# A depthwise-separable convolution on one core: pw in one transfer, x chunk 0 on ScalarE's queue, dummy matmuls up to pw's landing

## The chip, the cores and the metric

One core of a Trainium2 chip. The metric is the device time of an execution in microseconds. Two numbers occur: the **time** (575.14 us and so on), and the **span** of the same execution as its records show it. The time is 1.7 to 1.8 us longer than the span, so either can be used to compare kernels; I use spans where I take an execution apart.

## The reference

```python
H = W = 384; C = 384; k = 1                  # x: 1 x 384 x 384 x 384 bf16, dw: 1 x 1 x 384, pw: 384 x 384
out = xp[:, 0:H, 0:W, :] * dw[0, 0]          # k is 1: one scale for each channel
return jnp.einsum('bhwc,cd->bhwd', out, pw)
```

With k = 1 this is one matrix product, x (147,456 x 384) times diag(dw) pw. The kernel builds the weights w = diag(dw) pw once and then streams x through TensorE in 288 steps of 512 rows.

## The kernel before

The **prologue** makes the weights. dw is turned into a column by three tiny matmuls (L199), VectorE makes the scaled selection matrices `sel_w`, and TensorE multiplies them with pw (L218), in pairs of matmuls for the two halves of the rows. ScalarE and VectorE copy the six results from PSUM into `w_r`.

```python
nc.scalar.dma_start(dw_row[:], dw.rearrange("a e c -> a (e c)")).then_inc(s_dw, 16)
nc.sync.dma_start(pw_n[:, 0, :], pw[:P, :]).then_inc(s_pw[0], 16)
nc.sync.dma_start(pw_n[:, 1:3, :], pw[P:, :].rearrange("(k p) d -> p k d", p=P)).then_inc(s_pw[1], 16)
# ... then all loads of x and all stores, on the same SyncE queue, in the order in which they are due

nc.tensor.wait_ge(s_zero, 1)
idle_work(3)                      # dummies: 3 rounds of 4 matmuls on zeros, in a loop (L184)
# ... the three dw matmuls (L199)
idle_work(1)
times = {(1, 1): 3, (2, 0): 3}    # these build steps are repeated, only to keep TensorE busy
for k in range(3):
    if k < 2:
        nc.tensor.wait_ge(s_pw[k], 16)
    nc.tensor.wait_ge(s_sw, k + 1)
    for r in range(2):
        if k == 2:
            nc.tensor.wait_ge(*w_done[r])         # PSUM is used again: a copy must be done
        for v in [0, 1] * times.get((k, r), 1):
            mm = nc.tensor.matmul(...)            # L218: sel_w x pw_n
        mm.then_inc(s_w)
```

The **loop** has 48 matmuls a step (L167), after VectorE has transposed the rows of x and with ScalarE evicting the step before. And the last three loads of x have another layout, whose first dimension is only 4:

```python
if first + LONG < NS:                              # LONG = 3
    src = rows.rearrange("(p s) c -> p (s c)", p=P)
    dst = dst.rearrange("p s c -> p (s c)")
else:
    src = rows.rearrange("(a k q) c -> q a k c", k=4, q=4)
```

## Time and profile before

| | before |
|---|---|
| time, first three runs | 575.14 us (574.9 to 576.55) |
| span of the profiled run | 574.1 us |
| prologue, up to the loop's first matmul | 7.28 us |
| first eviction, last eviction | 9.80, 569.45 us |
| tail, last eviction to the end | 4.7 us |
| DMA, mean over the span | 395 GB/s |

The lines that carry this stand in the prediction below. Here are rows of the stretches of 1 us at the end of the kernel before, and SyncE's last wait for the stores. The last two figures of a stretch are the busy share of the 16 DMA engines and what they moved in GB/s.

```profile
571.00:572.00 1.00, 0.00 (x0) 0.00 (x0) 0.00 (x0) 0.00 (x0) 0.00 (x0) 1.00 0.68 267
572.00:573.00 1.00, 0.00 (x0) 0.00 (x0) 0.00 (x0) 0.00 (x0) 0.00 (x0) 1.00 0.32 126
573.00:574.00 1.00, 0.00 (x0) 0.00 (x0) 0.00 (x0) 0.00 (x0) 0.00 (x0) 1.00 0.00 0
```

```profile
SPq L142 <- DMA out_dram<-O: 2.0, 1, 2.0
```

No engine computes here any more. The last store drains at hundreds of GB/s, then nothing is left, and SyncE has waited 2.0 us for it. In this run the end was clean.

### The profile page before, as it was taken

The numbers are of one execution on the slowest core, as the hardware profiler recorded it, in microseconds if no ns is written. First come the engines' busy times: TensorE is split into PE (matmuls) and PEld (weight loads), VectorE is DVE, ScalarE is ACT, GpSimd is POOL, SyncE is SP. The second block draws the span as 40 slices with busy tenths as digits, with TensorE's granted clock in tenths as the row PEclk, the third lists the DMA queues.
The fourth block names the chain that finished last, engine by engine and source line by source line (L and its number), as shares of the span: only waits on it lengthen the run. The fifth ranks groups of instructions, "written<-read, shape, count | busy, mean of one in ns | idle before, by whom it ended". The sixth has DMA issues, their size and how long they took to land.

```text
span 574.1 us, 29692 instructions
## 1 busy us (share of the span) xinstructions
PE 567.5 (99%) x13863; PEld 334.3 (58%) x13863; DVE 508.2 (89%) x583; ACT 419.1 (73%) x296; POOL 0.9 (0%) x8
## 2 busy tenths in 40 slices
PE   8999999999999999999999999999999999999996
PEld 4555555555555555555555555555555555555553
DVE  7889888988988898899889888988988898899884
ACT  6777777777777777777777777777777777777775
POOL 0000000000000000000000000000000000000000
PEclk9999999999999999999999999999999999999999
DMA  8999999999999999999999999999999999995996
GB/s 327 442 404 408 431 415 423 436 429 405 383 411 412 391 400 428 398 390 402 426 385 400 398 430 403 390 393 419 396 395 424 400 388 392 421 397 172 414 386 241
DMA packets 25929, 226.88 MB, mean 395 GB/s; under 512 B 1214, under 2 KB 5695, under 8 KB 22079
## 3 DMA queue, kind: packets, MB, share of 16 engines
q1 hardware_dynamic: 25916, 226.79, 98.1%
q14 instruction: 10, 0.07, 0.0%
q8 instruction: 1, 0.02, 0.0%
q10 hardware_dynamic: 2, 0.00, 0.0%
HBM read 113.54 MB, written 113.25 MB: 395 GB/s over the span
## 4 chain that ended last, share of the span: by engine, by line
PE 98%; DMA 1%; ACT 0%; DVE 0%; SPq 0%; issue 0%
PE ps L167 97%; DMA pw_n<-in_pw_dram 1%; PE ps L218 0%; DMA out_dram<-O 0%; ACT O L309 0%; DVE O L306 0%; SPq L132 0%; SPq L339 0%; SPq L100 0%
## 5 line engine op out<-in xcount | busy, mean ns | idle before, releaser
L167 PE MATMUL ps<-w_r,T 32*128 32x384 bf16 x13824 | 562.2, 321 | 0.0
L260 DVE STREAM_TRANSPOSE T<-X 128x384 uint32<-128x384 uint32 x576 | 505.0, 878 | 56.0 <-DMA X<-in_x_dram 1.4
L309 ACT CAST O<-ps 128x1536 bf16<-128x1536 f32 x288 | 413.6, 1436 | 148.1 <-PE ps L167 148.1
L167 PEld LDWEIGHTS ps<-w_r,T 32*128 32x128 bf16 x13824 | 332.5, 93 | 229.9 <-issue 1.0
L273 ACT CAST w_r<-ps 128x768 bf16<-128x768 f32 x5 | 3.9, 800 | 1.5 <-PE ps L218 1.5
L218 PE MATMUL ps<-pw_n,sel_w 64*128 64x384 bf16 x20 | 3.6, 518 | 0.5 <-DVE sel_w L288 0.3
L306 DVE CAST O<-ps 128x768 bf16<-128x768 f32 x1 | 1.0, 957 | 3.0 <-DMA out_dram<-O 3.0
L184 PE MATMUL ps<-zero 32*128 32x384 bf16 x16 | 1.8, 493 | 1.4 <-POOL zero L234 1.4
L218 PEld LDWEIGHTS ps<-pw_n,sel_w 64*128 64x128 bf16 x20 | 1.2, 131 | 2.6 <-DMA pw_n<-in_pw_dram 1.5
L246 ACT ACT_TABLE_LOAD x1 | 1.3, 1283 | 1.5 <-SPq L100 1.5
L278 DVE TENSOR_REDUCE sel<-eye 128x64 f32<-128x128 bf16 x1 | 0.3, 289 | 1.8 <-POOL eye L236 1.8
L184 PEld LDWEIGHTS ps<-zero 32*128 32x128 bf16 x16 | 0.5, 99 | 2.0 <-issue 2.0
L273 DVE CAST w_r<-ps 128x768 bf16<-128x768 f32 x1 | 1.0, 958 | 0.5 <-PE ps L218 0.5
L288 DVE TENSOR_SCALAR sel_w<-sel,dw_f 128x256 bf16<-128x256 f32 x3 | 0.9, 350 | 0.0
L285 DVE COPY dw_f<-ps 128x3 f32<-128x3 f32 x1 | 0.2, 160 | 0.8 <-PE ps L199 0.8
L236 POOL TENSOR_SCALAR_AFFINE_SELECT eye<-ones 128x128 bf16<-128x128 bf16 x1 | 0.3, 292 | 0.1
L246 ACT COPY warm<-warm 128x1 f32<-128x1 f32 x2 | 0.3, 189 | 0.0
L199 PEld LDWEIGHTS ps<-ones,dw_row 1*128 1x128 bf16 x3 | 0.2, 100 | 0.2 <-issue 0.2
L234 POOL MEMSET zero<- 128x192 uint32 x1 | 0.3, 258 | 0.0
L199 PE MATMUL ps<-ones,dw_row 1*128 1x1 bf16 x3 | 0.2, 160 | 0.0
L235 POOL MEMSET ones<- 128x128 bf16 x1 | 0.2, 204 | 0.0
L328 POOL MEMSET const-bfloat16-1.0<- 128x1 bf16 x1 | 0.1, 102 | 0.0
(4 smaller groups left out, 0.4 us busy)
## 6 DMA issues: line engine op xcount, KB each, us to landing
X<-in_x_dram SPq DMA_DIRECT2D x26, 3840.0 KB, 21.6
out_dram<-O SPq DMA_DIRECT2D x26, 3840.0 KB, 27.6
X<-in_x_dram SPq DMA_DIRECT2D x2, 1536.0 KB, 17.2
out_dram<-O SPq DMA_DIRECT2D x2, 1536.0 KB, 13.8
X<-in_x_dram SPq DMA_DIRECT2D x3, 768.0 KB, 7.6
out_dram<-O SPq DMA_DIRECT2D x3, 768.0 KB, 10.7
X<-in_x_dram SPq DMA_DIRECT2D x1, 2304.0 KB, 19.4
out_dram<-O SPq DMA_DIRECT2D x1, 2304.0 KB, 11.3
```

The costliest lines, as they stand in the source:

```text
L167: mm = nc.tensor.matmul(PS[s][:, q, :D], lhsT=Ts[s][32 * q : 32 * q + 32, b, par::2], rhs=w_r[32 * q : 32 * q + 32, b, par, :], start=(b, ...
L184: nc.tensor.matmul(PS[0][:, i, :D], lhsT=zero[32 * i : 32 * i + 32, 0:P], rhs=zero[32 * i : 32 * i + 32, :], start=True, stop=True, tile_p ...
L199: mm = nc.tensor.matmul(PS[1][:, 0, D + k : D + k + 1], lhsT=dw_row[:, P * k : P * k + P], rhs=ones[0:1, 0:1], start=True, stop=True,)
L218: mm = nc.tensor.matmul(PS[(k + 1) % 2][:, 2 * r + v, :D], lhsT=sel_w[64 * v : 64 * v + 64, k, r, :, :].rearrange("p q w -> p (q w)"), rhs ...
L234: nc.gpsimd.memset(zero[:].bitcast(U32), 0).then_inc(s_zero)
L236: nc.gpsimd.affine_select(out=eye[:], in_=ones[:], pattern=[[-1, P]], compare_op=mybir.AluOpType.is_equal, fill=0.0, base=0, channel_multi ...
L246: c = nc.scalar.copy(warm[:, s + 1 : s + 2], warm[:, 0:1])
L260: ins = nc.vector.transpose(out=Tw[:, 3 * h : 3 * h + 3], in_=Xw[:, :, j, 96 * h : 96 * h + 96].rearrange("p k (b w) -> p b k w", w=32),)
L273: o = nc.vector.tensor_copy(out, in_) if e == 0 else nc.scalar.copy(out, in_)
L288: nc.vector.tensor_scalar_mul(sel_w[:, k], sel[:].unsqueeze(2).to_broadcast([P, 2, 4, 32]), dw_f[:, k : k + 1]).then_inc(s_sw)
L306: e = nc.vector.tensor_copy(Ov[:, nq:4, j, :], PS[s][:, nq:4, :D])
L309: a = nc.scalar.copy(Ov[:, 0:nq, j, :], PS[s][:, 0:nq, :D])
```

## The change

Its intent: save one DMA issue on SyncE, start x earlier on a second queue, and fill TensorE's gaps before pw lands, in the hope that TensorE's clock comes up sooner. What I call the clock is read in two ways that agree: the trace's record of the granted clock begins at 8.08 us in the profile before, and the loop's matmuls take 485 ns each at 7.95 to 8.1 us and 321 ns from 8.5 on.

```diff
-    s_pw = [nc.alloc_semaphore(f"s_pw{h}") for h in range(2)]
+    s_pw = nc.alloc_semaphore("s_pw")
@@
-        def load_x(t):
+        def load_x(t, eng=nc.sync):
@@
-            nc.sync.dma_start(dst, src).then_inc(s_x[g % NR][i], 16)
+            eng.dma_start(dst, src).then_inc(s_x[g % NR][i], 16)
@@
-        nc.sync.dma_start(pw_n[:, 0, :], pw[:P, :]).then_inc(s_pw[0], 16)
-        nc.sync.dma_start(pw_n[:, 1:3, :], pw[P:, :].rearrange("(k p) d -> p k d", p=P)).then_inc(s_pw[1], 16)
+        load_x(0, nc.scalar)
+        nc.sync.dma_start(pw_n[:], pw.rearrange("(k p) d -> p k d", p=P)).then_inc(s_pw, 16)
@@
-            todo.append((g_end[g - NR] if g >= NR else -1, load_x, t))
+            if t > 0:
+                todo.append((g_end[g - NR] if g >= NR else -1, load_x, t))
@@
-        idle_work(1)
-        times = {(1, 1): 3, (2, 0): 3}
+        idle_work(3)
+        nc.tensor.wait_ge(s_pw, 16)
+        times = {(1, 1): 3, (2, 0): 2}
         for k in range(3):
-            if k < 2:
-                nc.tensor.wait_ge(s_pw[k], 16)
```

## The prediction

The sum stands: a third each of -0.6, +1.3 and 0.0 us, a mean of about +0.2, shaded towards the gain, which takes 575.14 to 575.1. Rival two's landing at 5.4 to 5.8 and its 1.1 us were the author's estimate.

The rest is read from the profile before. A busy TensorE is not one at its peak: it was busy for all of 7.6 to 8.0 us with 12 matmuls and for all of 8.4 to 8.8 with 20. "Cold" is a pair of L218 every 0.32 us, full clock the loop's 162.5 ns a round. The 0.2 us ahead of ScalarE's copy are those from the end of the first pair behind pw, 4.54 + 0.32 = 4.86, to the copy's start at 5.08. What is said per DMA engine (60 to 72 ns a row, 24 rows, 168 ns a packet) is estimated from the counted packets and busy shares, taking the packets as spread evenly over the 16 engines. And "the clock's phase" means no more than that the rise comes at another time in each run, 5.70 to 9.07 us in the fourteen profiles.

> **What bounds the kernel now.** I read the page's chain of waits first, to see which engine owns the end of the span.
>
> ```profile
> span 574.1 us, 29692 instructions
> PE 98%; DMA 1%; ACT 0%; DVE 0%; SPq 0%; issue 0%
> L167 PE MATMUL ps<-w_r,T 32*128 32x384 bf16 x13824 | 562.2, 321 | 0.0
> L309 ACT CAST O<-ps 128x1536 bf16<-128x1536 f32 x288 | 413.6, 1436 | 148.1 <-PE ps L167 148.1
> ```
>
> Nearly all of the chain is TensorE on one line, the main loop (L167), and the last column of its row says that TensorE had no idle time ahead of those matmuls. A busy TensorE need not be at its peak, so the pace must be checked another way. ScalarE evicts once per step of 512 rows and always waits for TensorE, so its start times are a clock for the loop. Here are the first two and the last two evictions in the timeline of ScalarE:
>
> ```profile
> 9.80 1.44 ACT L309 CAST O<-ps 128x1536 bf16<-128x1536 f32 x1 [1.30 <-PE ps L167]
> 11.75 1.44 ACT L309 CAST O<-ps 128x1536 bf16<-128x1536 f32 x1 [0.51 <-PE ps L167]
> ...
> 567.50 1.44 ACT L309 CAST O<-ps 128x1536 bf16<-128x1536 f32 x1 [0.51 <-PE ps L167]
> 569.45 0.80 ACT L309 CAST O<-ps 128x768 bf16<-128x768 f32 x1 [0.51 <-PE ps L167]
> ```
>
> From 9.80 to 569.45 are 287 steps: (569.45 - 9.80) / 287 = 1.950 us each, the same as the first gap. A step has 48 matmuls, four at a time, so 12 rounds of 162.5 ns. The loop therefore never stalls, on DMA or anything else, and nothing in this change touches it. The tail after the last eviction is 574.1 - 569.45 = 4.65 us and is not touched either. **Only the prologue, up to 7.28 us, and the pace of the first step are open to the change.** The chain in order of time shows who owns the prologue:
>
> ```profile
> 1.01 0.39 SPq L132
> 1.41 0.06 issue
> 1.47 3.03 DMA pw_n<-in_pw_dram
> 4.49 0.05 issue
> 4.54 2.74 PE ps L218 x12
> 7.28 558.25 PE ps L167 x11413
> ```
>
> The second pw transfer (192 KB) is issued at 1.47 and lands at 4.50. Then come eight pairs of weight-building matmuls (L218) of about 0.32 us, 2.74 us in all, and the loop starts at 7.28. Two neighbours nearly tie with that. In the timeline:
>
> ```profile
> 6.04 0.80 ACT L273 CAST w_r<-ps 128x768 bf16<-128x768 f32 x1 [0.16 <-PE ps L218]
> 6.24 18.09 DVE L260 STREAM_TRANSPOSE T<-X 128x384 uint32<-128x384 uint32 x20 [0.84 <-DMA X<-in_x_dram]
> ```
>
> The loop's first matmul needs ScalarE's third weight copy, done at 6.84, and the first half of the transposed x, done at 6.24 + about 0.87 = 7.11. So if pw were 1 us earlier but x were not, only some 0.15 us would be won.
>
> [...] 0.32 us per L218 pair, 162.5 ns per round in the loop. [...] queried in short stretches, L167 matmuls average 485 ns at 7.95 to 8.1, 385 at 8.1 to 8.25 and 321 from 8.5, so the clock came up near 8.15, and the stretch before it without a gap began at 4.54, 3.6 us earlier. The page's PEclk row shows full speed throughout, so it does not record this. [...]
>
> **The change part by part.**
>
> *pw as one transfer.* It is issued at 1.01 instead of 1.01 and 1.47, which saves SyncE one issue (0.42 us). But the DMA engines were not starved: from 2.0 to 3.2 us they moved 321 packets, 72 to 83% busy, nearly all of pw's 768-byte rows; that is 16 x 1.2 / 321 = 60 to 72 ns per row and engine. 384 rows are 24 per engine, 1.5 to 1.7 us, so pw's bytes end near 3.6 in either form, and the last semaphore came 0.9 us later, at 4.50. The single transfer may land at 4.0 to 4.5 if nothing else shares the engines. What is lost is the early start on the first third: before, that third landed at 3.0 and its two pairs (0.64 us) and one ScalarE copy (0.80 us) ran while the rest was in flight. Now all nine pairs follow the landing.
>
> *Nine pairs for ten.* (2,0) repeats twice instead of three times. Cold: 9 x 0.32 = 2.88 us after pw, against 2.74 before. ScalarE's third copy: six pairs x 0.32 = 1.92, about 0.2 for the drain and semaphore, 0.80 for the copy: pw + 2.95. If the clock were already full, the pairs would take 9 x 0.16 = 1.46, but the three copies in a row, at 0.96 each from start to start (5.08 and 6.04 in the trace), plus some 0.4 ahead of the first, end at pw + 3.1. Either way **the loop starts at about pw + 3.0**. With pw at 4.3 that is 7.3: the same as now.
>
> *x chunk 0 from ScalarE.* It is issued behind dw at about 1.49 instead of 1.92, and the later chunks move up two SyncE issues, some 0.9 us. Its landing may move from 6.2 to between 5.2 and 5.8, so the transpose is off the path. ScalarE's table load (1.28 us) slips by 0.45 to about 2.0 to 3.3, still before its first copy: hidden.
>
> *Two more dummy rounds of the loop.* The L184 rounds start 0.43 us apart (1.40, 1.84, 2.27, 2.71). Three instead of one end at 2.71 + 3 x 0.43 = 4.0. They are free if pw lands after that, and their purpose is the clock: TensorE then has no gap from 1.4 to 4.0, where before it had one of 0.33 and one of 0.42.
>
> What the clock is worth: the first step would end in 1.95 us at full clock. The first eviction came at 9.80; counted back from it at full clock, the loop would have begun at 9.80 - 11 x 0.1625 - 0.32 - 0.05 = 7.64. It began at 7.28, so the cold rounds cost 0.36 us in this run. [...] Earlier activity could save 0.4 us[...].
>
> **The rivals.** One: *the wanted gain* - pw lands near 4.2, no gap, clock up before the loop: start 7.2, no cold rounds, 0.4 to 1.0 us faster. For it: the near-continuous activity. [...] Two: *a new wait in place of the old one* - x chunk 0, now on a second queue[...]. Its packets of 3 KB took about 168 ns per engine (114 packets in the stretch 3.6 to 4.8)[...], pw lands at up to 5.4 to 5.8, TensorE idles 1.4 us or more after its dummies, and the loop starts at 8.4 or later: 1.1 us lost[...]. For it: x followed pw in the same queue before[...]. Against it: the DMA engines were not full on small rows, so a second queue may fill their pauses. Three: *no net change* - pw lands at 4.4 to 4.6, the serial nine pairs eat the saved issue, start 7.4 to 7.6, and the clock gives the 0.3 back. A fourth, that earlier x loads speed the loop later, is excluded by the 1.950 us pace.
>
> **Range and chances.** I give about a third to each: -0.6, +1.3 and 0.0, mean about +0.2; that the dummies were evidently tuned to a landing near 4.0 makes me shade it towards the gain. From 575.14 I predict 575.1. The spread of the clock's phase (1.65 us over three runs) goes on top: 573.9 to 576.4. Two per cent is 11.5 us, more than the whole prologue of 7.3 us, so faster by 2% cannot follow from this change; slower by 2% would need a stall in the loop that nothing here points to.
>
> **What would show it.** pw's time to landing: 3.0 to 3.5 us from an issue at 1.01 for rivals one and three, 4.3 or more for rival two. L218's idle time on pw: under 0.5 us, or over 1.2. The start of L167 minus pw's landing: 3.0. The wait of the transposes on x should no longer reach past 6. The L167 matmuls' mean in the first 2 us says when the clock came up: 321 ns from the first on proves the dummies. The evictions must stay 1.95 us apart; if they do not, I have missed something in the DMA traffic. I would be wrong on the total if the loop's start moved by more than 1.5 us either way, and on the mechanism if the clock came up early without pw being on time.

## More of the kernel before

Stores and loads share one queue, whose packets take 98.1% of the time of the 16 DMA engines (q1 on the page of the kernel before), and run at 395 GB/s on average over the span.

## The result, and the profile after

Over six runs each the changed kernel took 575.68 us (575.39 to 577.51) and the kernel before 576.16 (574.9 to 576.55). The ratio is 1.0001, 95% interval 0.9985 to 1.0018. Ratios here are the mean time of one kernel's runs over that of the other's of the same rounds, so they are not quite the ratio of the two medians. No difference is established.

The profiled run of the changed kernel has a span of 575.8 us, 1.7 longer than the profile before, and yet its loop was *earlier*. First its chain in order of time, cut to the prologue and the loop:

```profile
1.01 3.00 DMA pw_n<-in_pw_dram
4.02 0.05 issue
4.07 0.52 PE ps L218 x2
4.58 0.02 issue
4.61 2.24 ACT w_r L273 x3
6.85 0.14 issue
6.99 555.96 PE ps L168 x13680
```

pw lands at 4.02 instead of 4.50. The loop (now L168) starts at 6.99 instead of 7.28, and what it waits for has changed hands: ScalarE's three copies in a row (L273), no longer TensorE's own build matmuls. Why not those is seen in the L218 group of two short stretches, 5.3 to 5.6 and 6.1 to 6.5 us (the second figure after the bar is the mean in ns):

```profile
L218 PE MATMUL ps<-pw_n,sel_w 64*128 64x384 bf16 x4 | 0.8, 518 | 0.0
...
L218 PE MATMUL ps<-pw_n,sel_w 64*128 64x384 bf16 x6 | 0.7, 322 | 0.0
```

The same matmul goes from 518 to 322 ns: TensorE's clock came up in between. The trace file's record of the granted clock (no view prints its start) begins at 5.70 us; in the profile before it begins at 8.08. So here the first step ran at full clock (321 to 323 ns a matmul from 7.3 us on), and the first eviction came 0.64 us sooner. In the timeline of ScalarE:

```profile
9.16 1.44 ACT L309 CAST O<-ps 128x1536 bf16<-128x1536 f32 x1 [0.92 <-PE ps L168]
...
568.81 0.80 ACT L309 CAST O<-ps 128x768 bf16<-128x768 f32 x1 [0.51 <-PE ps L168]
```

(568.81 - 9.16) / 287 is again 1.950 us, so the loop kept the 0.64 us to its last step. They were lost after it: from 568.81 to 575.8 are 7.0 us, where the kernel before took 4.7. The stretches of 1 us at the end, and SyncE's last wait, show on what:

```profile
571.00:572.00 1.00, 0.00 (x0) 0.00 (x0) 0.00 (x0) 0.00 (x0) 0.00 (x0) 1.00 0.75 298
572.00:573.00 1.00, 0.00 (x0) 0.00 (x0) 0.00 (x0) 0.00 (x0) 0.00 (x0) 0.66 0.15 54
573.00:574.00 1.00, 0.00 (x0) 0.00 (x0) 0.00 (x0) 0.00 (x0) 0.00 (x0) 0.50 0.06 25
```

```profile
SPq L143 <- DMA out_dram<-O: 4.2, 1, 4.2
```

At the very end the DMA engines move only 54 and then 25 GB/s, with a mean busy share of 0.15 and then 0.06 of 16 engines. That is the work of two or three engines (0.15 x 16 = 2.4) and then of about one (0.06 x 16 = 1.0): I read it as **stragglers** that still move the stores while the others are done, which is not shown, as the trace has only the sum over the engines. SyncE waits 4.2 us. The profiled run was the longest of the six; the other five spans are 573.7 to 574.3.

Two questions follow. Is the prologue's gain real on average, or was it the time at which the clock happened to come up? And is the tail part of the change, or noise that hides it?

### The profile page after: what moved, and what is told of

Read it like the earlier page. It is cut to its first block, busy times and chain, and to the rows that moved or that the text cites. A ratio compares the mean times of both kernels' runs of the same rounds, so it can differ in the third digit from the quotient of the medians.

```text
span 575.8 us, 29706 instructions
## 1 busy us (share of the span) xinstructions
PE 566.8 (98%) x13869; PEld 414.7 (72%) x13869; DVE 506.6 (88%) x583; ACT 419.0 (73%) x296; POOL 0.9 (0%) x8
## 4 chain that ended last, share of the span: by engine, by line
PE 97%; DMA 1%; ACT 1%; DVE 0%; issue 0%; SPq 0%
PE ps L168 97%; DMA out_dram<-O 1%; DMA pw_n<-in_pw_dram 1%; ACT w_r L273 0%; ACT O L309 0%; DVE O L306 0%; PE ps L218 0%; SPq L339 0%; SPq L100 0%
## 5 line engine op out<-in xcount | busy, mean ns | idle before, releaser
L168 PE MATMUL ps<-w_r,T 32*128 32x384 bf16 x13824 | 561.8, 321 | 0.5 <-ACT w_r L273 0.5
L168 PEld LDWEIGHTS ps<-w_r,T 32*128 32x128 bf16 x13824 | 412.9, 93 | 149.4 <-issue 0.9
L273 ACT CAST w_r<-ps 128x768 bf16<-128x768 f32 x5 | 3.6, 805 | 1.1 <-PE ps L218 1.1
L218 PE MATMUL ps<-pw_n,sel_w 64*128 64x384 bf16 x18 | 2.4, 434 | 0.1
L218 PEld LDWEIGHTS ps<-pw_n,sel_w 64*128 64x128 bf16 x18 | 1.1, 124 | 1.4 <-issue 0.9
L273 DVE CAST w_r<-ps 128x768 bf16<-128x768 f32 x1 | 1.0, 958 | 1.0 <-PE ps L218 1.0
```

The lines of the kernel that those rows point to most:

```text
L168: mm = nc.tensor.matmul(PS[s][:, q, :D], lhsT=Ts[s][32 * q : 32 * q + 32, b, par::2], rhs=w_r[32 * q : 32 * q + 32, b, par, :], start=(b, ...
L218: mm = nc.tensor.matmul(PS[(k + 1) % 2][:, 2 * r + v, :D], lhsT=sel_w[64 * v : 64 * v + 64, k, r, :, :].rearrange("p q w -> p (q w)"), rhs ...
L273: o = nc.vector.tensor_copy(out, in_) if e == 0 else nc.scalar.copy(out, in_)
```

## The experiments

My theory was that the prologue gain is real and is hidden by a DMA backlog at the end. The rivals were that the change lengthens the tail itself, and that it gains nothing in the prologue on average. Experiments named "light" are compared by the mean span of their six runs.

### The two kernels again

`aa_before` is the kernel before, unedited, timed against itself; `after_again` is the changed kernel, unedited.

> The kernel before against itself, to see what the timing alone does. Every theory expects a ratio within 0.3% of 1, single spans between 573.2 and 575 us as so far (the spread of 1.65 us between equal programs), and evictions 1.95 us apart in the profile. How much of the spread comes from the start (when TensorE's clock comes up[...]) and how much from the tail (4.6 to 7 us after the last eviction) is what the profile adds.

> The changed kernel again. Theory (the prologue's gain is real and the tail hid it in the profiled run): first eviction again near 9.2 us, 0.5 to 0.7 us before that of the kernel before; most spans at 573.4 to 574.3, 0.3 to 0.9 us under the kernel before, one in six or so longer by 1.5 us or more, with a tail of over 6 us after the last eviction. Rival (the change itself makes the tail longer, because x starts earlier and meets the stores otherwise): the tail is over 6 us here too, and the spans average the same as the kernel before.

The kernel before against itself gave 1.0 (0.9987 to 1.0013). The changed kernel gave 1.0005 (0.9993 to 1.0017), with a mean span of 574.5 us beside 574.0 of the eleven runs of before. The expected 0.3 to 0.9 us gain was a miss. Its profile had the first eviction at 9.45 and `aa_before` had it at 9.44: the difference of 0.64 us between the first two profiles did not come back, as the clock came up at 7.54 and 7.66 us this time. The tails were 6.6 and 5.6 us. So the first theory was half down. The rival's forecast for `after_again`, a tail of over 6 us and spans that average the same, did come true.

### The last three loads cut in four

Those loads move at 77 to 113 GB/s from 521 to 530 us of the profile before, about a quarter of the usual rate, with the DMA engines 33 to 38% busy. I took this for a few engines that carry them alone, which no run shows, and the backlog of stores behind them for the cause of the tail. The cut, made in both kernels (`before_tail16`, `after_tail16`):

```diff
-            nc.sync.dma_start(dst, src).then_inc(s_x[g % NR][i], 16)
+            if first + LONG < NS:
+                nc.sync.dma_start(dst, src).then_inc(s_x[g % NR][i], 16)
+            else:
+                for q in range(4):
+                    nc.sync.dma_start(dst[32 * q : 32 * q + 32], src[q]).then_inc(s_x[g % NR][i], 16)
```

> The kernel before with the last three loads of x cut in four each by q, so that their first dimension is 32 and not 4; the data are the same. Theory: [...] (the DMA row falls to a third for about 12 us from 517 on at about 100 GB/s), and the backlog of stores behind them is what makes the tail vary. Expected: no such lull, the x loads issue without blocking SyncE for 5 to 12 us, the tail after the last eviction is 4.4 to 4.8 us, and the spread of spans shrinks to that of the start (1.7 us at most). If the tail has another cause, it stays as spread out as in the kernel before.

> The same cut of the last three loads on the changed kernel. If the tail hid the gain, this shows it bare: spans 573.2 to 574.0 with no outlier at 575 or more, and 0.4 to 1.0 us under before_tail16, 0.1 to 0.2% under the kernel before. If the change makes the tail longer by itself, the spans stay where after_again has them.

Both expectations failed. The spans grew to a mean of 576.1 (before) and 575.9 us (after), ratios 1.0037 (1.0023 to 1.005) and 1.0033 (1.0021 to 1.0045), both with tails of 7.0 to 7.1 us. The end of `before_tail16`, in stretches of 1 us:

```profile
571.00:572.00 1.00, 0.00 (x0) 0.00 (x0) 0.00 (x0) 0.00 (x0) 0.00 (x0) 1.00 0.84 330
572.00:573.00 1.00, 0.00 (x0) 0.00 (x0) 0.00 (x0) 0.00 (x0) 0.00 (x0) 1.00 0.07 28
573.00:574.00 1.00, 0.00 (x0) 0.00 (x0) 0.00 (x0) 0.00 (x0) 0.00 (x0) 0.76 0.06 25
```

Again one engine's worth at 25 GB/s, for longer. But the edit did not do what it was meant to do: the slow stretch was still there. Here is `before_tail16` from 505 to 580 us, in 40 slices of 1.9 us (busy tenths, then GB/s):

```profile
DMA  9999999974005799999999999989928879550000
GB/s 414 447 413 432 413 407 412 262 178 119 32 27 145 238 391 449 397 426 422 406 438 410 406 401 410 406 351 371 398 86 324 313 278 358 221 222 25 0 0 0
```

So these two runs do not decide whether the slow stretch makes the tail. What I overlooked at first is how long SyncE takes to issue those loads, the last two of five 6.36 and 5.14 us in the kernel before and 11.75 and 4.43 us in the changed kernel, and with it the store behind them. SyncE's stores from there on, in the two in that order:

```profile
525.14 45.70 SPq L128 DMA_DIRECT2D out_dram<-O  x9
...
529.12 41.09 SPq L128 DMA_DIRECT2D out_dram<-O  x9
```

That store goes out at 525.1 us in the profile before (tail 4.7), at 527.6 in `dummies_o8` below and 527.9 in `aa_before` (both 5.6), at 529.0 and 529.1 in `after_again` and the changed kernel (6.6 and 7.0), and at 529.4 and 529.6 in the two runs with the cut (7.1 and 7.0). The later the stores resume, the longer the tail. This is the order that my theory of a backlog asks for, but no run moved this store alone, so it is not shown to be the cause. A late start alone is not the whole of it either: the slice of `before_tail16` from 559.4 to 561.3 us has 86 GB/s at two tenths busy, so most of the engines' time was free by then. What is shown is that the end follows the DMA engines' work and not TensorE's: first evictions of 9.31 and 9.22 us, as good as any, ended 2 us later than the kernel before.

### Lighter stores: the same two kernels without the backlog

Each of the 26 big stores leaves out a quarter of its rows, 25.6 MB of 227. The result is wrong; the arithmetic on the engines stays the same.

```diff
+                if L == LMAX:
+                    dst, src = dst[:, 0:3], src[:, 0:3]
```

> The kernel before with each 3840 KB store cut to three of its four quarters (wrong result on purpose), so that the DMA engines have some 11% less to do and can clear their backlog. Theory (what is left on a straggling DMA engine sets the end): no packets at 20 to 40 GB/s after the bulk is through, a tail of 4.5 to 4.8 us after the last eviction in every run, spans then first eviction + 559.65 + 4.65, that is 573.3 to 574.5 by when the clock comes up. If the tail stays between 5 and 7 us, the backlog isn't what makes it. The result is incorrect by design.

> The changed kernel with the same lighter stores (wrong on purpose). Theory (prologue gain real, hidden by the DMA backlog at the end): spans 0.25 to 0.6 us under light_before, the first eviction at 9.15 to 9.5 us. Rival (the change gains nothing in the prologue on average, the first two profiles differed by the clock's phase only): spans within 0.1 us of light_before.

The tail is now 4.7 and 4.8 us, and in the profiles of all seven light kernels it lies between 4.68 and 4.82, where the seven profiles with full stores had 4.7 to 7.1. SyncE's last wait in `light_before`:

```profile
SPq L144 <- DMA out_dram<-O: 2.0, 1, 2.0
```

So it is the stores that make the tail long. With less of them, the two kernels can be compared bare, and they show **no difference**: `light_before` 573.75 us on average (573.2 to 574.2), `light_after` 573.77 (573.5 to 574.1). By the scatter of the six runs each, an estimate, the difference is known to within some 0.4 us. The forecast of my theory, 0.25 to 0.6 us gained, was missed, and the rival "nothing gained in the prologue on average" stands within that interval. The profiles agree as to the loop's start: four of the kernel before with its own prologue have it at 6.96 to 7.28 us, mean 7.10, four of the changed kernel at 6.99 to 7.18, mean 7.06. Does no part do anything, or do the parts cancel?

### The parts, each alone and each undone

All with light stores. `light_dummies` is the kernel before with the dummy part alone (which also runs nine pairs of build matmuls for ten), `light_pw_one` has pw as one transfer alone, `light_x_act` has x chunk 0 on ScalarE's queue alone; `light_after_idle1` is the change without its two extra dummy rounds, `light_after_x_sync` the change with x back on SyncE's queue.

```diff
# light_dummies, against light_before
-        idle_work(1)
-        times = {(1, 1): 3, (2, 0): 3}
+        idle_work(3)
+        times = {(1, 1): 3, (2, 0): 2}
# light_pw_one, against light_before
-        nc.sync.dma_start(pw_n[:, 0, :], pw[:P, :]).then_inc(s_pw[0], 16)
-        nc.sync.dma_start(pw_n[:, 1:3, :], pw[P:, :]...).then_inc(s_pw[1], 16)
+        nc.sync.dma_start(pw_n[:], pw.rearrange("(k p) d -> p k d", p=P)).then_inc(s_pw, 16)
-            if k < 2:
-                nc.tensor.wait_ge(s_pw[k], 16)
+            if k == 0:
+                nc.tensor.wait_ge(s_pw, 16)
# light_x_act, against light_before (and load_x with an engine, as in the change)
+        load_x(0, nc.scalar)
         nc.sync.dma_start(pw_n[:, 0, :], pw[:P, :]).then_inc(s_pw[0], 16)
# light_after_idle1, against light_after
-        idle_work(3)
+        idle_work(1)
# light_after_x_sync, against light_after
-        load_x(0, nc.scalar)
         nc.sync.dma_start(pw_n[:], ...).then_inc(s_pw, 16)
+        load_x(0)
```

> The kernel before with only the dummy part of the change (three rounds, and two repeats in place of three of the third build step), stores lighter as above. If the dummies alone carry the gain: spans as in light_after, 0.25 us or more under light_before. If they need the other parts: the dummies end at about 4.05 and hold back the first third of pw, so the loop starts at 7.2 to 7.4 as before and the spans equal light_before within 0.1 us or are longer.

> The kernel before with pw as one transfer and one wait alone (ten pairs, one round of dummies, x as before), stores lighter (wrong on purpose). Theory (this part costs: the first third of pw no longer lands early, so all ten pairs follow the landing at about 4.0): TensorE idles from 3.2 to about 4.05, the loop starts at 7.2 to 7.4[...]; mean span 0.2 to 0.6 us over the 573.75 of light_before. Rival (one issue less is a gain): mean span at or under 573.7.

> The kernel before with x chunk 0 issued by ScalarE alone, stores lighter (wrong on purpose). If x on the second queue competes with pw: the second pw transfer lands 0.2 us or more later than the 4.0 to 4.5 so far, and the span is longer by that. If the queue is free: x's first transpose starts no later than 5.9, pw lands as before, and the mean span is within 0.15 us of light_before (573.75), because the loop's start is set by pw's matmuls and not by x.

> The changed kernel with one round of dummy matmuls instead of three ahead of pw's landing, stores lighter as above. If the dummies bring the clock up sooner: clock up later[...] (profile: matmuls at 485 ns still after 8 us in some runs), spans 0.2 to 0.6 us over light_after. If they do nothing: same as light_after within 0.1 us.

> The changed kernel with x chunk 0 back on SyncE's queue behind pw, stores lighter (wrong on purpose): what the x part is worth inside the change. If x on ScalarE's queue delays pw there too, as it did alone (the second pw transfer landed 4.0 us after its issue instead of 3.0): pw now lands at 3.8 or earlier, and the span is at or under the 573.77 of light_after. If x on ScalarE's queue is a gain inside the change: x lands some 0.4 us later here, the first transpose starts at 6.2 instead of 5.8, the loop cannot start before 7.1, and the mean span is 0.05 to 0.3 us over light_after. TensorE's dummies end at 4.0 in either case.

| kernel (light stores) | mean span, us | range | loop starts | clock up |
|---|---|---|---|---|
| light_before | 573.75 | 573.2 to 574.2 | 6.97 | 8.49 |
| light_dummies | 573.53 | 573.5 to 573.6 | 7.04 | 6.82 |
| light_pw_one | 574.62 | 573.9 to 575.2 | 7.57 | 8.43 |
| light_x_act | 575.77 | 575.0 to 576.5 | 8.23 | 9.07 |
| light_after_idle1 | 574.23 | 573.7 to 575.0 | 7.28 | 7.64 |
| light_after_x_sync | 573.85 | 573.6 to 574.2 | 7.04 | 7.32 |
| light_after | 573.77 | 573.5 to 574.1 | 7.18 | 6.98 |

Loop starts and clock times are those of the one profiled run each. Before, dummies, after and idle1 ran on one chip; pw_one and x_act on another, x_sync on a third, so I lean on their chains as well as on their means. A difference of two of these means is known to within some 0.4 to 0.7 us (0.2 for `light_after` against `light_dummies`, which scatter little), again an estimate from the scatter of six runs each.

*pw as one transfer, alone, costs.* The mean span is 0.9 us longer, more than the 0.2 to 0.6 expected. The chain of `light_pw_one`:

```profile
1.01 3.13 DMA pw_n<-in_pw_dram
4.14 0.05 issue
4.19 3.38 PE ps L219 x20
7.57 558.28 PE ps L168 x13716
```

All of pw lands at 4.14. In `light_before` the second of the two transfers landed 2.5 us after its issue at 1.47, at about 4.0, but that was one of the earliest: in the six profiles with two transfers and x behind them it landed at 4.0 to 4.6, mean 4.2, and in the seven with one transfer pw landed at 3.8 to 4.1, mean 4.0. So the saved issue bought some 0.2 us. But the first third no longer lands early, and all twenty matmuls (3.38 us) stand behind the landing: they start at 4.19, in `light_before` at 3.59. These 0.6 us, at the loop's start 7.57 beside 6.97, are what the chain shows of the 0.9; the rest is within the scatter (574.62 - 573.75 is known to some 0.6 us).

*x on the second queue, alone, costs 2.0 us.* The chain of `light_x_act`:

```profile
1.47 3.98 DMA pw_n<-in_pw_dram
5.44 0.05 issue
5.49 2.74 PE ps L222 x16
8.23 558.27 PE ps L171 x13071
```

The second pw transfer takes 3.98 us to land instead of 2.5 to 3.1. Its issue began at 1.47, and ScalarE's x went out at 1.52: the two were on their way together, and pw lost. The loop starts 1.3 us later than in `light_before`; the rest of the 2.0 us goes with the later clock (9.07) and the scatter. Inside the change the same x costs nothing: there pw goes out as one transfer at 1.01, half a microsecond ahead of x, and lands at 3.8 to 4.1 with or without it (`light_after` and `light_after_x_sync`, 573.77 and 573.85, no difference beyond their scatter). That it is this lead which protects pw fits, but no run varied the lead alone. Nor does x gain anything there. It landed at 5.3 to 5.6 us from ScalarE's queue and at 5.1 and 5.5 from SyncE's behind a single pw transfer. In both cases it was there before the first transpose (5.84 in `light_after`, 5.69 in `light_after_x_sync`), which no longer waits for x but for VectorE's own copy of weights.

*The dummies gain a little: 0.2 us with the pair fewer, 0.5 us inside the change.* Neither mean is clear of the scatter by itself, and the first lies just under the 0.25 us asked for. `light_dummies` starts its loop no earlier than `light_before`, but the clock is up before it:

```profile
2.85 1.18 PE ps L186 x12
4.02 2.96 PE ps L220 x18
6.98 0.06 issue
7.04 557.90 PE ps L169 x13728
```

Its six spans lie within 0.1 us of each other, where `light_before` spreads over 1.0 us, and that is clear. Over all fourteen profiles, the seven kernels with one dummy round ahead of the pw matmuls had the clock up at 6.9 to 9.1 us, mean 8.0; the seven with three rounds at 5.7 to 7.5, mean 6.8. The clock rises at another time in each run (the changed kernel had 5.70 and 7.54 in its two profiles), so single profiles prove nothing, but the two groups differ by 1.3 us, and by 1.0 without `light_pw_one` and `light_x_act`, in which TensorE also idled longer (its matmuls and weight loads sat idle for 2.3 and 3.5 us until pw landed, in `light_before` for 1.0).

So the parts work and cancel, as far as these means carry: the change gives away 0.6 to 0.9 us by the single transfer, gets some 0.8 us of it back by the dummies and the one pair fewer (574.62 for `light_pw_one`, 573.85 for `light_after_x_sync`, on different chips), and its x part is worth nothing. The parts do not simply add. With three dummy rounds TensorE is taken until 4.02 in any case, so the early third of pw is worth less: on one chip `light_after` is only 0.24 us behind `light_dummies`.

### A version meant to beat both

The dummies alone, full stores and a correct result, and one load of 1536 KB near the end given a first dimension of 8. I hoped that this would keep it off some of the engines and spare each of them some 96 KB, a sixteenth of it (3.8 us, an estimate from the 25 GB/s above), the straggler among them. No run shows that the first dimension decides which engines carry a load, nor how many carried this one.

```diff
+                if len(groups[g]) == 2 and i == 1:
+                    src = rows.rearrange("(o p s) c -> o p (s c)", o=8, p=P // 8)
```

> A version meant to beat both, with all stores and a correct result: of the change only the dummies, and one 1536 KB load of x near the end issued with a first dimension of 8[...]. Theory (one straggling engine[...] is some 2 us behind at the end[...]): if the straggler is among the spared, the tail is 4.7 us in every run, spans 573.4 to 573.7, 0.3 us or more under the kernel before. If it is among the other half: the tail grows by up to 3.8 us, spans at 576 or more.

It did not beat them: ratio 1.0005 (0.9986 to 1.0024), mean span 574.4 us beside 574.2 of the kernel before. Its prologue was as good as that of `light_dummies` (first eviction 9.21), but the tail of the profiled run was 5.6 us, with SyncE's last wait at

```profile
SPq L144 <- DMA out_dram<-O: 2.9, 1, 2.9
```

Neither of the two expected outcomes came: the tail is not clean, and it has not grown by 3.8 us. It is that of `aa_before`, where the stores resume at about the same time, so the layout of this load left no mark that I can see. Two of six spans were 573.6, two over 575. The trace has only sums over the 16 engines, so which engine straggles, and whether it is always the same, stays open.

## Why the prediction was right or wrong

The time was right: 575.1 us predicted, 573.9 to 576.4 as the range, 575.68 measured. There is luck in it. The forecast was the mean of three outcomes thought about equally likely, and the one profile behind it had pw landing (4.49) and x landing (6.22) later than most and the shortest of the seven tails. Of its steps:

- **The loop never stalls: right.** 1.950 us between evictions before and after.
- **pw's landing gains little from the single transfer: right.** Expected at 4.0 to 4.5, it came at 3.8 to 4.1; two transfers had it at 4.0 to 4.6, so some 0.2 us were gained.
- **The loop starts at pw + 3.0: right, with one addition.** 6.99 - 4.02 = 2.97 in the changed kernel, and by ScalarE's three copies, as the second branch of that step had it when the clock is up. Its parts were off and made up for each other: 0.59 us ahead of the first copy for 0.4, and 0.75 a copy (2.24 / 3) for 0.96. In `after_again` pw landed at 3.8, before the dummies ended at 4.02, and the 3.0 us count from that end: there the extra rounds were not free. The early start on the first third of pw was worth 0.6 us at the loop's start (`light_pw_one`), which the step named but did not put a figure on.
- **Rival three, no net change: right, in substance.** "The serial nine pairs eat the saved issue, and the clock gives the 0.3 back" is what the parts show, with 0.6 to 0.9 lost and some 0.8 given back: larger parts, the same sum. Its loop start of 7.4 to 7.6 was too late; the four profiles have 6.99 to 7.18.
- **Rival two, x in competition with pw: a real effect, but not in this change.** It cost 2.0 us when x was added alone, and pw then landed at 5.44, within the 5.4 to 5.8 of the estimate; how the packets of the two queues followed one another is not shown. The step failed in expecting the same of the change; there pw is issued half a microsecond ahead and landed by 4.1.
- **The dummies bring the clock up sooner: right in direction.** The clock rose at 6.8 us instead of 8.0, means of seven profiles each, but the mean worth is 0.2 to 0.5 us, at or under the lower end of the 0.4 to 1.0 of rival one. The prediction says that the page does not record the clock: PEclk is 1.00 even in stretches of 0.4 us before 8 us, but the trace's record begins at 8.08, close to the 8.15 worked out from the matmuls.
- **x's earlier landing: right, and of no use.** It was to move from 6.2 to 5.2 to 5.8, and from ScalarE's queue it landed at 5.3 to 5.6 in the change. But x on SyncE's queue landed at 5.5 to 6.2 in the kernels with two pw transfers, so 6.2 was a late one, and with x early the transposes waited for VectorE's weight copy instead, to 5.7 to 5.9.
- **"The tail after the last eviction is 574.1 - 569.45 = 4.65 us and is not touched either": the step that failed.** With full stores it is 4.7 to 7.1 us, from one run to the next, and adds up to 2.4 us of work that the DMA engines still have to do. The same mistake is in putting the spread of 1.65 us down to the clock's phase. With the tail clean, the kernel before still spreads over 1.0 us and `light_dummies` over 0.1; the rest is the tail. A DMA share of 98.1% stood on the page. I took the steady evictions as proof that DMA does not matter, and they prove it only up to the last eviction.

Whether the change lengthens the tail a little by itself stays open. Its two profiles had 7.0 and 6.6 us, those of the kernel before 4.7 and 5.6, with stores that resumed at 529 beside 525 and 528, but the timed runs don't separate them (1.0001 and 1.0005, both with 1 well inside the interval).

## What to carry to other kernels

When two resources are both near 100% (here TensorE 99% and DMA 98.1%), the one that sets the pace of the loop does not have to set its end: look at the last microseconds for a DMA rate that falls to that of one engine (here 25 GB/s), and at when the last stores were issued, and make the DMA lighter in a throw-away kernel before crediting a small gain or loss to anything else. In the prologue, try to issue a transfer on the critical path clearly ahead of any bulk transfer on another queue (here 0.05 us of lead went with a late landing and 0.5 us with none). Splitting it so that work can start on its first part can be worth more than the issue it costs (here 0.6 us at the loop's start against some 0.2). Undo the parts of a change one by one even when the sum is zero: here one part alone lost 0.6 to 0.9 us, another won most of it back. And check in the profile that a throw-away edit did what it was meant to do: here the cut loads left the slow stretch in place.
